# RWKV-7 and a hard-swish feed-forward on one core: unit 4's r loaded later, unit 8 prepared one block later

## The chip, the cores and the metric

The kernel runs on one core of a Trainium2 chip. The metric is the device time of one execution in microseconds (us). A measurement is the median of several runs; the profile is of one further execution.

## What is computed

First a recurrence over 768 steps for each of 4 x 8 heads of 40 features, then a feed-forward over the 3072 rows that it gives. The state is a 40 x 40 matrix for each head.

```python
for t in range(S):                     # B, H, S, D = 4, 8, 768, 40
    y[:, :, t] = einsum('bhd,bhde->bhe', r[t], state)
    Sa = einsum('bhde,bhe->bhd', state, a[t])
    state = state * w[t] - Sa (outer) b[t] + v[t] (outer) k[t]
x = y.transpose(0, 2, 1, 3).reshape(B * S, H * D)         # 3072 x 320
h = x @ w_in                                               # 320 -> 2048
out = (h * clip(h + 3, 0, 6) / 6) @ w_out                  # 2048 -> 320
```

## The kernel before

**Units and groups.** The sequence is cut into chunks of 64 steps. A unit is one chunk of one pair of batches with all 8 heads: 24 units, numbered 0 to 23, in six groups of four (`NU = 4`). Within a chunk the recurrence is written as matrix products, which needs the inverse of a triangular 64 x 64 matrix for each head.

**Preparation of a unit** (`prepare`): stages that do not need the state. `W` turns w on TensorE (L506), evicts it (L595, L599) and scans it on VectorE (L603); `gam` makes the cumulative products and their reciprocals (L612 to L635). `A` and `B` turn a and b and scale them (L528 or L506, L516, L650, L658). `F` is the matrix to be inverted (L672 or L685, evicted at L676 or L692 and L695). `factor` turns the reciprocals (L705, L710), evicts them as rgt (L714, L717), and GpSimd scales k and b by them (KBt, L725). `K`, `E`, `EV` follow (L736, L554 with the mask L578, L752 with the eviction L757).

**Inversion** (`invert`): for each group, some 60 small VectorE instructions (L804, L810) on all four units' F, two transposes (L813, L818), and copies into tinv (L825, L826). The other 32 x 32 blocks come from matrix products, two per half group (`third_block`: L839, evicted at L847, then L862, evicted at L872).

**A unit's own step** (`step`): `RT`, `VT` (r and v turned: L531 and L516), `fade` (the state decays, L913), `R` (L927, L931), `C` (L554, L578), `S` (L949), `U`, `UT` (L968, L1007), `rS` (L1023), `H`, `ysn` (L1064, then L1071 to L1074: outputs and the new state), `move` and `move2` (DMAs of the outputs into xt, L1111 and L1116).

**Feed-forward** (`feed_forward`): 48 jobs, two for each unit. `expand` computes h (L1171; L1184 in another shape), the activation makes gt (L1193 on ScalarE, L1194 on VectorE), `contract` computes o (L1219), and ob goes to memory (L1243). These jobs are dealt out in pieces (`pieces`, `feed`) between the stages of the recurrence. Each engine runs its instructions in the order in which the program writes them down, so where a piece stands is fixed.

**Loads.** `fetch` issues a unit's loads on SyncE's queue: two DMAs for W, B or K (L490), four for V (L487), and for r of unit 4 and later eight and for a of unit 8 and later four (L478). A load is written down where the tile that it overwrites has been read for the last time: W of the next unit in the stage `W`, A in `A`, B and K in `factor`, r of the next unit in `RT`. Units from 8 on share one tile for each of W, A, B and K. SyncE handles its queue in order; an instruction that waits holds up those behind it.

**Order.** (1) The first group is prepared, and the matrices w_in and w_out are loaded and converted. (2) `PLAN` is a list of lines by hand: the steps of units 0 to 3. From its line 10 (`BEGIN`) the second group, units 4 to 7, is prepared beside it by the generator `by_twos`, one `next` per line; its remaining rounds are run after the plan. (3) The inversion of the second group is finished under 18 rounds of 1.25 feed-forward pieces each. (4) From then on the units 4 to 23 each take four blocks; blocks are counted from `m = 0`. Unit 4's `RT` and `VT` stand ahead of block 0, unit 5's in block 3; `R`, `C`, `S` of unit 4 are in block 1, `U`, `UT`, `rS` in block 2, `H` in block 3, `ysn` in block 4, `move` in block 5; and so on, four blocks later for each unit.

In (4) `begins` gives the block in which the preparation of a unit starts. Where the next unit's preparation starts less than four blocks later, the five blocks are

```python
    CLOSE_STAGES = [["W", "gam"], ["A", "B"], ["F", "K", "factor"], ["E"], ["EV"]]
```

`a_block(m)` sorts what is due in block m into two parts: own steps, and preparations that started in a block divisible by 4, go into the first; the other preparations go into the second. Half of the block's feed-forward pieces stand between the parts and half behind them. The third-block products of a group (`block`) stand behind the second part of the first two blocks of its first and of its second unit: L839 in the one, L862 in the other.

`together` runs a part: first the TensorE halves of all its stages, in the order of `PRODUCTS`, then the remaining halves (evictions, VectorE and GpSimd work, loads) in the order of `RESULTS`. PSUM for this is one single bank (`one`) and two pairs of banks (`pair`), which stages share as far as their widths allow (512 columns a bank); if a part needs more than five banks, what has begun is finished first.

```python
    PRODUCTS = ["W", "S", "K", "VT", "B", "factor",
                "ysn", "EV", "R", "C", "U", "UT", "rS", "H", "E", "F"]
    RESULTS = ["ysn", "W", "VT", "EV", "R", "S", "C", "A", "B", "move", "move2", "open",
               "U", "UT", "rS", "F", "K", "fade", "H", "E", "factor", "RT", "gam"]
```

Of the kernel before, what the change touches and what calls it, by code (L numbers as in the profile page):

```python
# [31 lines left out]
def kernel(  # L32
# [47 lines left out]
    NU = 2 * NP  # L80
# [30 lines left out]
    def begun_ffn():  # L111

        lent.__exit__(None, None, None)
        pairs.clear()
        pairs.append(("pair", 2))
        pools["h"] = ctx.enter_context(tc.tile_pool(name="hidden", bufs=1, space=PSUM))
# [70 lines left out]
    AHEAD, FAR = NU + 1, 2 * NU - 1  # L187
# [6 lines left out]
    def second(name):  # L194

        tag = {"B": "S", "K": "U"}[name]
        return padded(grp.tile([P, H, SLOT], F32, name=name + "1", tag=tag, bufs=1), name)

    def seconds():
        t = inv.tile([P, 2, H, SLOT], F32, name="WA1", tag="x", bufs=1)  # L200
        for i, name in enumerate("WA"):
            others[name] = padded(t[:, i], name)
# [244 lines left out]
    NK = NG * NU  # L447
# [3 lines left out]
    def fetch(name, i, engine=None):  # L451

        if i is None or i >= NK:
            return
        x, crossed = {"W": (w, 0), "A": (a, 0), "B": (b, 0), "K": (k, 0), "R": (r, 1),
                      "V": (v, 1)}[name]
        if name == "V":
            t = values[i % AHEAD]
        else:
            t = placed.get((name, i))  # L460
            if (name, i) == ("R", 1):
                t = others["K"]
            if (name, i) == ("W", NU + 1):
                t = values[NU]
            t = t if t is not None else (others if i < 2 * NU and i % 2 and name != "R" else inputs)[name]
        g, p = names[i]
        engines = engine or nc.sync
        if name == "R" and i >= NU or name == "A" and i >= 2 * NU:
            y = x[2 * p:2 * p + 2, :, g * BL:(g + 1) * BL, :]
            n = 2 if name == "R" else 1  # L470
            y = y.rearrange("q (k s j) t e -> s j (q k) (t e)", s=2, j=n).rearrange(
                "s j k (l e) -> s j l k e", e=2 * D)
            for s in range(2):
                for c in range(0, D, L):
                    z = s * SLOT + c
                    to = rooms[name][z:z + L].rearrange("l (j k e) -> l j k e", j=n, e=2 * D)
                    for j in range(n):
                        nc.sync.dma_start(out=to[:, j, :, 0:2 * D - c], in_=y[s, j, :, :, c:])  # L478
            data[i][name + "N"] = t
            return  # L480
        for q in range(2):
            engine = engines[q] if isinstance(engines, tuple) else engines
            y = x[2 * p + q, :, g * BL:(g + 1) * BL, :]
            rows = slice(q * BL, (q + 1) * BL)
            if crossed:
                for s in range(2):
                    engine.dma_start(out=t[rows, 4 * s:4 * s + 4, 0:D],  # L487
                                     in_=y[s::2].rearrange("h t e -> t h e"))
            else:
                engine.dma_start(out=t[rows, :, 0:D], in_=y.rearrange("h t e -> t h e"))  # L490
        data[i][name + "N"] = t
# [761 lines left out]
    def pieces(n):  # L1253

        owed[0] += n * (8 / 9 if spread[0] else 1)
        while owed[0] >= 1:
            owed[0] -= 1
            if not next(stream):
                owed[0] = 0.0

    def aside(n, weight=0):

        for _ in range(n):
            if side and next(side[0], side) is side:
                side.popleft()
            due[0] += weight
            while due[0] >= 1:
                due[0] -= 1
                next(weights, None)
# [6 lines left out]
    def run(stage, steps=0, mixed=0, deals=0):  # L1276

        for at in stage:
            if at == DONE:
                return  # L1280
            aside(steps, mixed)
            deal(deals)
# [26 lines left out]
    def by_twos(first, steps, mixed, rate):  # L1309


        chains = [by_stages(first + i, prepared(first + i)) for i in range(NU)]
        for t in range(TWOS):

            order = [0, 1] if t < STAGES else []
            order += [2, 3] if t > 5 else []
            if t < 2:
                order = [0, 1, 0, 1][4 * t:]
            if t == 3:
                order = [2, 0, 3, 1]  # L1320
            for i in order:
                if t >= 2 or first != NU:
                    run(chains[i], steps if t > 10 else 0, mixed, 1 if t < 5 else 0)
                pieces(rate / 2)
            if t == 10:
                side.append(invert(group_F[-1], third, first == 0))
            yield
# [88 lines left out]
    for t, line in enumerate(plan):  # L1416
        if t == 8:
            begun_ffn()
            ring.clear()
            ring.extend([("one", 1), ("whole", 2)])  # L1420
        for name, *amounts in line:
            run(chains[name[0]], 0, 0, *map(int, amounts))
        limit[0] = {3: 15, 8: 17, 9: PIECES}.get(t, limit[0])
        if t == BEGIN - 2:
            seconds()
            third.clear()
            second_group = by_twos(NU, 3, 0, 1.25)
        if t == BEGIN:
            fetch("A", NU + 1)
            fetch("W", NU + 3)  # L1430
        if t == BEGIN + 2:
            fetch("V", NU)
            fetch("V", NU + 1)
            fetch("R", NU)
        if t == BEGIN + 1:

            for name in "BK":
                others[name] = second(name)
                fetch(name, NU + 1)
        if t >= BEGIN - 2:  # L1440
            pieces(3 if t < BEGIN else 1.5 if t < BEGIN + 3 else 0)
        if t >= BEGIN:
            next(second_group)
    for _ in weights:
        pass
    for _ in second_group:
        pass
    for _ in range(18):
        aside(3)
        pieces(1.25)  # L1450
# [18 lines left out]
    BLOCKS = 4  # L1469
# [33 lines left out]
                     for stage in stages[name])  # L1503
        finish()

    begins = {u: max(3 * (u - 2 * NU), BLOCKS * (u - NU - AHEAD)) for u in range(2 * NU, NK)}
    coming, ahead, own = deque(range(2 * NU, NK)), {}, {}

    def a_block(m):
# [95 lines left out]
```

## Time and profile before

| | before |
|---|---|
| median of 3 runs | 773.58 us (771.44 to 774.97) |
| the profiled execution | 772.7 us; its span, first to last instruction, 771.0 us |
| TensorE (PE) busy | 710.8 us, 92% |
| VectorE (DVE) busy | 508.8 us, 66% |
| ScalarE (ACT) busy | 310.4 us, 40% |
| GpSimd (POOL) busy | 150.8 us, 20% |
| mean granted TensorE clock | 0.956 of full speed |
| DMA | 48.43 MB in 175999 packets, mean 63 GB/s |

All positions below are microseconds from the start of the profiled span. The first two parts of the order above end at about 166 us, the third at about 190 us; the blocks fill the rest up to the last jobs. In rows of a timeline the columns are start, duration, engine, line, operation, what it writes and reads, shape and count; in brackets stands the idle time of the engine before it and what ended it. SPq is SyncE's queue; its rows are the issuing of DMAs, not their transfer.

### The profile page before, as it was taken

The page shows a single profiled execution, that of the slowest core. Times are in us where ns is not written, and L with a number is a line of the kernel's source. Part 1 is how long each engine was busy: PE and PEld are TensorE (multiplying, and loading weights), DVE is VectorE, ACT ScalarE, POOL GpSimd, SP SyncE. Part 2 cuts the span into 40 slices and gives each one's busy share as a digit, 9 for nine tenths or more (in the row PEclk, how much of TensorE's full clock was granted, in tenths as well). Part 3 has the DMA queues.
Part 4 walks back from the last instruction along what each step waited for, and adds up shares of the span by engine and source line. Part 5 has one row for each costly group of instructions (what it writes and reads, how often), then busy time and mean ns, then how long its engine had stood idle before and what let it go on. Part 6 is the DMA issues. An engine that isn't in the chain of part 4 may idle for free.

```text
span 771.0 us, 33034 instructions
## 1 busy us (share of the span) xinstructions
PE 710.8 (92%) x14568; PEld 603.1 (78%) x14568; DVE 508.8 (66%) x1027; ACT 310.4 (40%) x644; POOL 150.8 (20%) x303
## 2 busy tenths in 40 slices
PE   4635888999899989999999999999999999999997
PEld 3534777778779778888888888888888888888885
DVE  8899968588557799556798456898436982333210
ACT  2377865232553324552434453234444224322211
POOL 7403210321322211212112121203112010000000
PEclk7956799999999999999999999999999999999999
DMA  9685563420334322233322223313331110110000
GB/s 124 119 179 150 114 170 57 79 43 18 64 65 84 70 55 48 52 71 60 64 52 55 53 62 63 69 37 60 57 72 42 25 24 23 35 35 12 14 16 19
DMA packets 175999, 48.43 MB, mean 63 GB/s; under 512 B 159216, under 2 KB 174576, under 8 KB 175856
## 3 DMA queue, kind: packets, MB, share of 16 engines
q1 hardware_dynamic: 171552, 45.58, 29.7%
q8 instruction: 115, 1.88, 1.0%
q10 hardware_dynamic: 4304, 0.74, 0.7%
q14 instruction: 28, 0.23, 0.1%
HBM read 37.62 MB, written 3.93 MB: 54 GB/s over the span
## 4 chain that ended last, share of the span: by engine, by line
PE 77%; DVE 8%; SPq 5%; issue 3%; DMA 3%; ACT 3%; POOL 0%; DVEq 0%; ACTq 0%; POOLq 0%
PE o L1219 25%; PE h L1171 24%; PE pair L554 4%; PE pair L1064 4%; SPq L490 3%; PE h L1184 2%; PE one L506 2%; PE pair L968 2%; PE pair L927 1%; DVE prod L804 1%; PE pair L1007 1%; PE pair L516 1%; PE pair L752 1%; DVE x L810 1%; PE pair L1023 1%
## 5 line engine op out<-in xcount | busy, mean ns | idle before, releaser
L1171 PE MATMUL h<-xt,win 128*128 128x128 f32 (+1 forms) x2000 | 229.2, 282 | 3.0 <-DVE gt L1194 3.0
L1219 PE MATMUL o<-wout,gt 128*128 128x320 f32 x768 | 230.4, 443 | 0.0
L1171 PEld LDWEIGHTS h<-xt,win 128*128 128x128 f32 (+1 forms) x2000 | 212.9, 193 | 17.5 <-issue 3.1
L1219 PEld LDWEIGHTS o<-wout,gt 128*128 128x128 f32 x768 | 138.6, 190 | 50.3 <-issue 0.2
L1193 ACT ACTIVATE gt<-h,three 128x512 f32<-128x512 f32 x96 | 62.6, 686 | 110.3 <-PE h L1171 88.0
L1194 DVE SCALAR_TENSOR_TENSOR gt<-gt,h 128x512 f32<-128x512 f32 x96 | 61.8, 679 | 62.4 <-ACT gt L1193 62.3
L578 DVE COPY_PREDICATED area<-mask,pair 128x512 f32<-128x512 int32 x56 | 40.5, 726 | 55.2 <-PE pair L554 36.7
L804 DVE TENSOR_TENSOR prod<-x 128x30 f32<-128x30 f32 (+9 forms) x180 | 64.1, 356 | 8.9 <-POOL x L789 3.3
L810 DVE TENSOR_TENSOR x<-x,prod 128x30 f32<-128x30 f32 (+9 forms) x180 | 63.0, 350 | 5.5
L725 POOL TENSOR_TENSOR KBt<-K,rgt 128x320 f32<-128x320 f32 x22 | 19.1, 866 | 142.2 <-ACT rgt L714 134.2
L1071 DVE TENSOR_TENSOR ys<-pair,ys 128x512 f32<-128x512 f32 x20 | 13.8, 690 | 40.5 <-PE pair L1064 40.5
L993 POOL COPY area<-V 128x320 f32<-128x320 f32 x20 | 9.1, 454 | 149.6 <-DVE area L645 53.7
L757 ACT ACTIVATE EV<-pair 64x320 f32<-64x320 f32 x44 | 19.0, 432 | 39.2 <-PE pair L752 38.9
L1064 PE MATMUL pair<-area,KBt 64*64 64x104 f32 x1280 | 32.4, 250 | 0.0
L1237 ACT ACTIVATE ob<-o 128x320 f32<-128x320 f32 x22 | 9.6, 435 | 56.6 <-PE o L1219 35.2
L603 DVE TENSOR_TENSOR_SCAN prods<-area,start 128x528 f32<-128x528 f32 x24 | 29.9, 1250 | 3.4 <-ACT area L599 3.3
L632 POOL COPY gam<-prods 128x256 f32<-128x256 f32 x24 | 12.7, 531 | 99.1 <-DVE prods L603 99.1
L614 DVE TENSOR_TENSOR_SCAN area<-area,start 128x528 f32<-128x528 f32 x24 | 30.6, 1276 | 0.8
L1064 PEld LDWEIGHTS pair<-area,KBt 64*64 64x64 f32 x1280 | 29.9, 133 | 1.5 <-issue 1.4
L872 ACT ACTIVATE tinv<-pair 32x256 f32<-32x256 f32 x48 | 18.0, 375 | 31.9 <-PE pair L862 31.3
L931 DVE TENSOR_TENSOR RR<-pair,EV 128x320 f32<-128x320 f32 x22 | 10.7, 485 | 20.9 <-PE pair L554 13.6
L633 POOL COPY rgam<-prods 128x256 f32<-128x256 f32 x22 | 23.9, 1084 | 0.0
(289 smaller groups left out, 1078.5 us busy)
## 6 DMA issues: line engine op xcount, KB each, us to landing
V<-in_v_dram SPq DMA_DIRECT2D x96, 40.0 KB
out_dram<-ob SPq DMA_DIRECT2D x47, 80.0 KB
R<-in_r_dram SPq DMA_DIRECT2D x92, 40.0 KB
B<-in_b_dram SPq DMA_DIRECT2D x42, 80.0 KB
K<-in_k_dram SPq DMA_DIRECT2D x42, 80.0 KB
W<-in_w_dram SPq DMA_DIRECT2D x37, 80.0 KB
A<-in_a_dram SPq DMA_DIRECT2D x37, 80.0 KB
xt<-yg SPq DMA_DIRECT2D x72, 40.0 KB
```

What stands on the lines that cost most here:

```text
L554: nc.tensor.matmul(out=o[i][half(q), n ^ (2 * q * placed), :], lhsT=lhs[half(i, D), n ^ (2 * q * swap), half(q)], rhs=rhs[half(i, D), n, h ...
L578: nc.vector.copy_predicated(out=x[:].rearrange("p (i h) t -> p i h t", i=2), mask=mask8, data=o[2])
L603: nc.vector.tensor_tensor_scan(out=prods[:].rearrange("p r m i -> p (r m i)"), data0=wm[:, 0:SCAN], data1=start[:], initial=0.0, op0=ALU.m ...
L614: nc.vector.tensor_tensor_scan(out=back, data0=back, data1=start[:], initial=0.0, op0=ALU.mult, op1=ALU.add)
L633: nc.gpsimd.tensor_copy(rv[:, :, 0:HB], o["prods"][:, :, 0, 0:HB][:, :, ::-1])
L804: nc.vector.tensor_tensor(out=pv, in0=_ap(x[:], (i + 1) * L + i, [[L, n], [0, i]]), in1=_ap(x[:], i * L, [[0, n], [1, i]]), op=ALU.mult,)
L810: nc.vector.tensor_tensor(out=rest, in0=rest, in1=pv, op=ALU.add)
L1064: nc.tensor.matmul(out=both[q][half(s), pr, :], lhsT=o[name][half(q), h * D:h * D + SLOT], rhs=beside[name][half(q), 4 * rs + 2 * (s ^ (q ...
L1171: nc.tensor.matmul(out=hp[c][:, i, :], lhsT=lhsT, rhs=rhs, start=(begun[c] == 0), stop=(begun[c] == 3 * NQ - 1))
L1193: nc.scalar.activation(out=gt[:], in_=hp[c][:], func=AF.Relu, bias=three[:], scale=1.0)
L1194: nc.vector.scalar_tensor_tensor(out=gt[:], in0=gt[:], scalar=6.0, in1=hp[c][:], op0=ALU.min, op1=ALU.mult)
L1219: nc.tensor.matmul(out=op[:], lhsT=gts[c][:, n, :], rhs=wout[:, c * HJ + r * NQ + n, :], start=((split or r == 0) and c == 0 and n == 0), ...
```

## The change

Two edits. The load of r for unit 4 (`fetch("R", NU)`, eight DMAs) is taken from the plan's line 12, where it stood behind the loads of v for units 4 and 5, and is written down behind the last round of `by_twos`, ahead of the 18 rounds of feed-forward pieces. And `begins` of unit 8 becomes 1 instead of 0; those of the other units (3, 6, 9, 12, ...) stay. With that unit 8's five stages stand in blocks 1 to 5 and in their second parts (1 is not divisible by 4), instead of in the first parts of blocks 0 to 4.

```diff
         if t == BEGIN + 2:
             fetch("V", NU)
             fetch("V", NU + 1)
-            fetch("R", NU)
...
     for _ in second_group:
         pass
+    fetch("R", NU)
     for _ in range(18):
         aside(3)
         pieces(1.25)
...
-    begins = {u: max(3 * (u - 2 * NU), BLOCKS * (u - NU - AHEAD)) for u in range(2 * NU, NK)}
+    begins = {u: max(3 * (u - 2 * NU), BLOCKS * (u - NU - AHEAD), 1) for u in range(2 * NU, NK)}
```

## The prediction

> **What bounds the kernel now.** The page came first: TensorE is busy for 92% of the span and carries 77% of the chain that ended last. The second view, busy time in chosen stretches, says where TensorE's order alone decides. Columns: stretch and length, then busy time and count of PE, PEld, DVE, ACT, POOL, then granted clock, DMA share, GB/s.
>
> ```profile
> PE 77%; DVE 8%; SPq 5%; issue 3%; DMA 3%; ACT 3%; POOL 0%; DVEq 0%; ACTq 0%; POOLq 0%
> ```
>
> ```profile
> 147.42:150.83 3.41, 1.73 (x14) 1.37 (x13) 0.69 (x1) 0.48 (x2) 0.00 (x0) 1.00 0.58 98
> ...
> 161.07:164.48 3.41, 1.91 (x68) 1.56 (x68) 3.24 (x6) 0.49 (x2) 3.06 (x5) 1.00 0.13 24
> 164.48:167.90 3.42, 3.42 (x41) 2.48 (x40) 3.18 (x10) 1.23 (x3) 0.00 (x0) 0.50 0.46 80
> ...
> 277.12:280.54 3.42, 1.51 (x17) 1.32 (x20) 3.25 (x10) 0.00 (x0) 0.07 (x1) 1.00 0.00 0
> 280.54:283.95 3.41, 3.41 (x42) 3.13 (x43) 3.20 (x7) 1.92 (x4) 1.32 (x4) 0.50 0.38 81
> 290.00:758.00 468.00, 468.00 (x9381) 399.31 (x9380) 278.32 (x564) 171.73 (x372) 74.18 (x137) 1.00 0.23 46
> ```
>
> From 290 us on TensorE never stops, so its remaining work there is fixed, and the change can act only through TensorE's idle time before 290. The other pairs show that a stretch with TensorE idle for 1.5 to 1.9 us was twice followed by 3.4 us at half clock, and once (the first line, 1.7 us idle) not.
>
> Third, SyncE's and TensorE's timelines, and one row of the chain of waits, around what is moved.
>
> ```profile
> 129.51 3.93 SPq L478 DMA_DIRECT2D R<-in_r_dram  x8
> ...
> 144.12 1.35 SPq L490 DMA_DIRECT2D B<-in_b_dram  x2
> ...
> 146.94 1.90 SPq L490 DMA_DIRECT2D B<-in_b_dram  x2
> ...
> 163.82 1.27 SPq L490 DMA_DIRECT2D K<-in_k_dram  x2
> 177.16 11.11 SPq L1243 DMA_DIRECT2D out_dram<-ob  x4
> ```
>
> ```profile
> 148.21 2.59 DMA B<-in_b_dram
> ```
>
> ```profile
> 148.93 0.63 PE L506 MATMUL one<-ident,B 128*128 128x128 f32 x4 [1.30 <-DMA B<-in_b_dram]
> ...
> 150.93 0.63 PE L506 MATMUL pair<-ident,B 128*128 128x128 f32 x4 [0.48 <-DMA B<-in_b_dram]
> ...
> 199.84 0.75 PE L862 MATMUL pair<-zs,tt 32*32 32x32 f32 x64 [1.21 <-DVE area L645]
> ...
> 205.60 0.69 PE L1023 MATMUL pair<-RT,S 40*64 40x64 f32 x32 [1.10 <-ACT UT L1013]
> ...
> 212.43 0.60 PE L506 MATMUL one<-ident,W 128*128 128x128 f32 x4
> ...
> 218.42 0.46 PE L516 MATMUL pair<-ident,B 64*128 64x64 f32 x8
> ```
>
> SyncE issues almost without a pause from 124 to 158 us. Unit 4's r is in the middle of that, and TensorE waits 1.30 and 0.48 us for the b of units 6 and 7 issued behind it. The next two gaps, 1.21 and 1.10 us, lie in the first blocks of the second half, where unit 8's preparation stands. The last two rows are unit 9's W and b.
>
> **The r load.** Eight DMAs, 3.93 us of SyncE, leave the queue ahead of A, W, unit 3's xt moves, B, K and V. Everything behind comes up to 3.9 us earlier. What those loads wait for allows it: GpSimd's last read of the old b's (KBt, 136.63 and 138.33 us) is over before the new issue times, 140.2 and 143.0. Unit 7's b landed at 148.21 + 2.59 = 150.80; it will land near 146.9, and TensorE, with both gaps closed, asks for it at 149.1. So 1.78 us go and 2.3 us of slack remain; the work behind (transposes, F, then the inversion on VectorE up to 187.7) follows TensorE directly and shifts with it. **-1.8 us**, at worst 0 if other loads take the place.
>
> The load itself now stands behind unit 8's K (issued by 165.09) and ahead of the first output store, which sits in the queue until 177.16 for a contraction that starts at 172.08. SyncE is idle in between: issue near 165, 1.76 us from the last issue to landing (the chain's later R row), read at 194.71. 20 us of cover. Were it behind the stores instead (188.3), it would land near 194, still about in time. Cost nothing.
>
> **Unit 8, one block later.** Its stages keep their instructions, but move from the first half of blocks 0 to 4 (merged with unit 4's and 5's steps) to the second half of blocks 1 to 5 (merged with unit 9's preparation, which still begins at block 3).
>
> *What goes.* Unit 8's scans no longer stand on VectorE between RT (194.71) and the mask that frees the PSUM pair for L862 (199.07): the 1.21 us go. Without K and the factor transposes in front, U, UT and rS fit the five banks together, so rS need not wait for UT's eviction: 1.10 us go. **-2.3 us**, at worst 0.
>
> *The b of unit 9.* All units from 8 on share one b buffer. Unit 9's load is issued when unit 8's factor stage has read it. That was block 2, two blocks ahead of its use in block 4; now it is block 3. In TensorE's order from unit 9's W to unit 9's B stand, by starts in its timeline, W 0.44, K 0.53, the factor transposes 0.39, F 0.6, a feed-forward piece 1.18, ysn 1.47 and two pieces 2.35: asked for after 7.0 us. (Before, with other work between, 5.99, the last two rows above.) The load's path has prices from unit 9's own turn:
>
> ```profile
> 225.16 0.37 ACT L692 ACTIVATE F<-pair 32x256 f32<-32x256 f32 x1 [3.19 <-PE pair L685]
> ...
> 227.25 0.44 ACT L714 ACTIVATE rgt<-pair 128x320 f32<-128x320 f32 x1
> ```
>
> F's matmuls end 2.0 us after W begins; F's six evictions 2.1 (225.16 to 227.25), rgt 0.44, KBt twice 0.86, so the buffer is free at 6.3. Unit 6's r and unit 10's W are issued ahead of it, but they end by then. Two issues 1.35, landing 2.0 (unit 7's b) to 3.4 us (unit 6's: issued by 145.47, used at 148.93) after the second: 9.7 to 11.1, or 11.5 with one slow issue as in the 146.94 row. TensorE waits 2.7 to 4.5 us with all of its queue behind: unit 8's E, L839, the feed-forward pieces. I take **+3.0**, near the quicker landing since SyncE's neighbours there are few; below 0 it can't be.
>
> *Block 5.* Unit 8's EV now shares a PSUM pair with unit 9's factor transposes, which pushes F into the second pair. L862 of the next third block follows at once and needs one of the two: F's, free after EV's evictions (0.88, ScalarE's row at 216.21) and F's 2.1, or the other, after rgt. F's matmuls run 0.6 beside that: 0.88 + 2.1 - 0.6 + 0.1 for the hand-over. Before, F shared with the factor and L862 at 225.03 took a free pair. **+2.5 us**, from 0 (the allocator finds a free pair after all) to 2.9 (it picks the other).
>
> *The clock.* Two waits of 2.5 to 3.0 us are longer than those that twice brought the half clock. What the one from 164.48 cost, by TensorE's rows: a job's 48 h matmuls 5.51 instead of 4.83 (166.64 against 176.50), four o matmuls 1.88 instead of 1.34 (163.81 against 159.73), EV 1.09 instead of 0.68 (165.62 against 163.21): 1.6 us. Between 0 and two of them; I take one: **+1.6**. [...]
>
> Sum: -1.8 - 2.3 + 3.0 + 2.5 + 1.6 = +3.0 us. The profiled execution took 772.7 (span 771.0 and 1.7 around), 0.9 below the median of three, 773.58; what is added is the same on either: 775.7 and **776.6**. A measurement can tell about 0.5% here, 3.9 us, so this counts as no change.
>
> **Rivals.**
> *Late b with a slow clock twice (slower).* The same two waits, unit 9's b taking the long landing (4.5) and both waits followed by half clock (3.2): -4.1 + 4.5 + 2.5 + 3.2 = +6.1, 779.7. It decides from a b wait of 4 us on. For it: unit 6's landing of 3.4, the two half-clock rows. [...] 0.22.
> *The clock holds.* +1.4, 775.0. [...] 0.17.
> *One wait only.* If L862 finds a free pair, -4.1 + 3.0 and half a clock loss of 0.8: -0.3, 773.3. For it: the L862 before (199.84) waited for a mask alone although an older reader of the other pair was still to come, so the allocator chooses. 0.13.
> *The blocks have room (faster).* If unit 9's b also lands in time, nothing but gains: -4.1, 769.5. It needs the factor's chain of 6.3 us and the load's 3.4 to fit 7.0; the rows speak against it. 0.08.
> *The forecast* has the rest, 0.40, with its own range of +1.0 to +4.6 (774.6 to 778.2).
>
> **How the numbers follow.** Over 3.9 us slower: the first rival and a fifth of the forecast's share, 0.30. Over 3.9 us faster: most of the last rival and a little for gains that I don't see, 0.08. The rest, 0.62. The range from 770.5 to 780.0 leaves out the last rival and the worse half of the first, and takes in some spread of single runs (771.44 to 774.97).
>
> **What would show it.** Right: R (L478) issued near 163 and SyncE idle until the stores; no idle before L506 of B near 147; W (L506 one) of unit 8 after R and C, not before L839; L862 of the first third block and rS without a gap; then a gap at L516 of B, released by DMA, near 213 to 217, one of 2.5 us at the second L862, released by ACT; half clock behind one of them. Wrong: no gap at that L516 (the b path is shorter than I add up), no gap at L862 (other PSUM pairs), gaps left near 147, or any TensorE idle after 290.

## The result, and the profile after

| | before | changed |
|---|---|---|
| median, runs side by side | 772.73 us (5 runs, 770.95 to 774.97) | 780.6 us (5 runs, 778.2 to 780.95) |
| ratio, with its 95% interval | | 1.0092 (1.0065 to 1.012) |
| the profiled execution | 772.7 us, span 771.0 | 780.8 us, span 779.1 |

The change is slower, by 0.92%. A second measurement of the same kernel, further down, gave 1.0066 (1.0041 to 1.0092). The intervals overlap; the loss is 5 to 7 us by the two ratios. The forecast was +3.0 us, called no change; the measured 780.6 us lies just above the range of 770.5 to 780.0, nearest to the rival "late b with a slow clock twice".

The page's chain of work that ended last, shares by engine:

```profile
PE 73%; DVE 10%; SPq 6%; issue 5%; DMA 2%; ACT 2%; POOL 1%; DVEq 0%; POOLq 0%; ACTq 0%
```

TensorE's part of the chain fell from 77% to 73%. But this chain runs through the start of the kernel too, which differs by some us from one execution to the next (unit 4's A transposes begin at 124.82 us in the one profile and at 126.53 in the other, so 1.7 of the 8.1 us between the two spans lie ahead of both edits' places); the changed kernel without unit 8's edit also shows 73%, and it is not slower. So this line cannot carry the verdict, and the places are needed. SyncE's queue, the issuing of DMAs:

```profile
164.88 5.06 SPq L478 DMA_DIRECT2D R<-in_r_dram  x8
175.56 11.70 SPq L1243 DMA_DIRECT2D out_dram<-ob  x4
...
213.96 1.27 SPq L490 DMA_DIRECT2D B<-in_b_dram  x2
```

TensorE's timeline (the bracket is the idle time ahead of the row, and what ended it):

```profile
149.41 0.60 PE L506 MATMUL one<-ident,B 128*128 128x128 f32 x4
...
193.87 0.66 PE L949 MATMUL one<-ident,state 128*128 128x128 f32 x4 [0.42 <-DVE state L913]
...
197.26 0.75 PE L862 MATMUL pair<-zs,tt 32*32 32x32 f32 x64
...
200.90 0.65 PE L1023 MATMUL pair<-RT,S 40*64 40x64 f32 x32
...
207.34 0.60 PE L506 MATMUL one<-ident,W 128*128 128x128 f32 x4
...
216.73 0.29 PE L516 MATMUL pair<-ident,B 64*128 64x64 f32 x1 [2.11 <-DMA B<-in_b_dram]
217.27 0.68 PE L516 MATMUL pair<-ident,B 64*128 64x64 f32 x7 [0.24 <-DMA B<-in_b_dram]
...
230.33 1.03 PE L862 MATMUL pair<-zs,tt 32*32 32x32 f32 x64 [2.58 <-ACT F L695]
```

The r load stands at 164.88, behind K and ahead of the stores. The gaps ahead of the b of units 6 and 7, of the first L862 and of rS have gone; a small one of 0.42 us at the state is new. Two large ones have come: 2.11 and 0.24 us for unit 9's b, and 2.58 us at the second L862. ScalarE's rows ahead of that:

```profile
227.32 0.87 ACT L757 ACTIVATE EV<-pair 64x320 f32<-64x320 f32 x2 [3.39 <-PE pair L752]
...
229.63 0.65 ACT L695 ACTIVATE F<-pair 32x256 f32<-32x256 f32 x2
```

EV's evictions first, then F's, which end at 230.28; L862 begins at 230.33. The granted clock around the two waits (columns as in the prediction: PE, PEld, DVE, ACT, POOL, granted clock, DMA share, GB/s):

```profile
213.38:216.79 3.41, 1.30 (x6) 0.66 (x4) 2.78 (x6) 0.00 (x0) 1.87 (x4) 1.00 0.53 92
216.79:220.20 3.41, 3.17 (x105) 2.68 (x106) 1.05 (x2) 0.05 (x1) 0.00 (x0) 0.50 0.67 128
220.20:223.62 3.42, 3.42 (x24) 2.20 (x26) 0.27 (x1) 1.73 (x5) 0.00 (x0) 0.50 0.14 44
227.03:230.45 3.42, 0.83 (x61) 0.70 (x57) 0.00 (x0) 3.04 (x9) 0.00 (x0) 1.00 0.17 25
230.45:233.86 3.41, 3.41 (x69) 2.56 (x66) 0.49 (x1) 1.79 (x5) 2.35 (x4) 0.50 0.03 7
290.00:758.00 468.00, 466.28 (x9462) 397.43 (x9461) 282.81 (x578) 172.72 (x376) 74.15 (x137) 1.00 0.23 46
```

Each of the two waits is followed by half clock (0.50), the first by 6.83 us of it (216.79 to 223.62) and the second by 3.41 (230.45 to 233.86). The last line is not full: TensorE paused once for 1.72 us, at 326.50, where ScalarE also stood still (2.01 us) and the profile names no releaser. The prediction named any TensorE idle time after 290 us as a sign of being wrong. But in the second profile of the changed kernel TensorE is busy for all of 290 to 750, and one of the experiments (part 6, r at its old place) has a pause of 1.84 us at 317.80, ahead of the very same matmul: both have run 5794 matmuls by then. So the pause seems to belong to a place in the program and comes in some executions only; it is not taken for an effect of the change, and what holds TensorE there stays open.

**Where the time lies.** To leave out the start, the spans between fixed instructions of TensorE's timeline were compared: from the A transposes of unit 4 to the F of units 6 and 7 (the stretch of the r load), from there to VT of unit 4 (the last preparations and the third step of the order), from VT of unit 4 to U of unit 5 (blocks 0 to 5), and what follows to the end.

| kernel | unit 4's A to F of 6, 7 | F to VT of unit 4 | blocks 0 to 5 | rest |
|---|---|---|---|---|
| before | 29.53 | 35.97 | 37.74 | 542.90 |
| changed | 27.59 | 34.61 | 46.17 | 544.18 |
| changed, measured again | 27.59 | 34.61 | 46.56 | 542.30 |

So the first edit gives 1.9 us, and blocks 0 to 5 lose 8.4 to 8.8. The rest differs by 1.3 us, no more than the pause, so nothing of the loss is won back further on. The second column differs by 1.36 us, and that is luck of the profiles. A wait for a mask stands there in both, and only before is it followed by half clock (0.50 from 164.48 to 167.90, four o matmuls in 1.88 us instead of 1.34; in the changed kernel the granted clock is 1.00 from 160 to 190). The kernel before:

```profile
163.21 0.68 PE L752 MATMUL pair<-V,area 64*64 64x40 f32 x32 [1.50 <-DVE area L578]
163.81 1.88 PE L1219 MATMUL o<-wout,gt 128*128 128x320 f32 x4
```

The changed kernel:

```profile
162.95 0.68 PE L752 MATMUL pair<-V,area 64*64 64x40 f32 x32 [1.59 <-DVE area L578]
163.56 1.34 PE L1219 MATMUL o<-wout,gt 128*128 128x320 f32 x4
```

It does not follow r's place: with r at its old place that row takes 1.34 us in the first profile of the second edit alone and 2.50 us in its second, behind waits of 1.46 and 1.60 us.

### The profile page after: what moved, and what is told of

It reads as the page before. It is cut to its first block, busy times and chain, and to the rows that moved or that the text cites. A ratio compares the mean times of both kernels' runs of the same rounds, so it can differ in the third digit from the quotient of the medians.

```text
span 779.1 us, 33028 instructions
## 1 busy us (share of the span) xinstructions
PE 713.7 (92%) x14568; PEld 604.0 (78%) x14568; DVE 508.9 (65%) x1027; ACT 310.6 (40%) x644; POOL 149.5 (19%) x303
## 3 DMA queue, kind: packets, MB, share of 16 engines
q8 instruction: 115, 1.88, 1.0%
## 4 chain that ended last, share of the span: by engine, by line
PE 73%; DVE 10%; SPq 6%; issue 5%; DMA 2%; ACT 2%; POOL 1%; DVEq 0%; POOLq 0%; ACTq 0%
PE o L1219 24%; PE h L1171 23%; PE pair L554 4%; PE pair L1064 3%; PE h L1184 2%; DVE prod L804 2%; DVE x L810 2%; SPq L490 2%; PE one L506 2%; PE pair L927 2%; SPq L487 1%; PE pair L968 1%; PE pair L516 1%; PE pair L1007 1%; PE pair L1023 1%
## 5 line engine op out<-in xcount | busy, mean ns | idle before, releaser
L1219 PE MATMUL o<-wout,gt 128*128 128x320 f32 x768 | 233.6, 448 | 0.0
L1219 PEld LDWEIGHTS o<-wout,gt 128*128 128x128 f32 x768 | 140.6, 193 | 51.7 <-issue 2.2
```

Of the source, the lines that this page charges most:

```text
L1219: nc.tensor.matmul(out=op[:], lhsT=gts[c][:, n, :], rhs=wout[:, c * HJ + r * NQ + n, :], start=((split or r == 0) and c == 0 and n == 0), ...
```

## The experiments

The theory: the first edit gains as predicted; the second costs two waits, for unit 9's b and for a PSUM pair at the second L862, and each wait costs again through the half clock seen behind it. The rivals: the loss comes from the second parts of the blocks as such (what shares a part with what), not from the later start; or the waits only take time that is lost anyway further on; or the r load at its new place costs something. All ratios are against the kernel before, run on the same chip at the same time, in 5 rounds; the diffs are against the changed kernel.

**1. Each edit alone.** The first edit alone keeps `begins` as before:

```diff
-    begins = {u: max(3 * (u - 2 * NU), BLOCKS * (u - NU - AHEAD), 1) for u in range(2 * NU, NK)}
+    begins = {u: max(3 * (u - 2 * NU), BLOCKS * (u - NU - AHEAD)) for u in range(2 * NU, NK)}
```

> Only the first edit: unit 4's r loaded behind the second group's preparation; unit 8 begins at block 0 as before. Theory (all of the loss comes from unit 8's later start: two TensorE waits and the half clock behind them): the two gaps for the b of units 6 and 7 near 149 us are gone, nothing waits for r, 1.8 us faster than the kernel before, 771 where that takes 772.7. Rival (the late load of r costs something in the blocks, or shifts the loads behind it): no gain or slower, 773 to 776, with TensorE or VectorE waiting for a DMA between 165 and 230 us.

Measured: 772.46 us, ratio 0.9974 (0.9955 to 0.9993). The gaps for the b of units 6 and 7 are gone, those at the first L862 and at rS (1.20 and 1.10 us) are still there, no new wait appears. The second edit alone puts the load back:

```diff
             fetch("V", NU + 1)
+            fetch("R", NU)
...
-    fetch("R", NU)
```

> Only the second edit: unit 8 begins at block 1; unit 4's r stays where it was. Theory: the whole loss and none of the gain, the changed kernel plus 1.8: 782.4, some 9.7 above the kernel before, with a gap of 2 to 3 us at unit 9's B (released by DMA), one of 2.6 at the second L862 (released by ScalarE's F), and half clock behind them. Rival (the two edits do it together, unit 4's r being late in SyncE's queue): within 2 us of the kernel before.

Measured: 780.32 us, 1.0063 (1.004 to 1.0087), +5.4 us by the medians where +9.7 was expected. Its profile has both waits (2.06 + 0.36 and 2.59 us) and half clock behind both, and 46.12 us in the blocks. The places were right and the sum too large; whether the two edits add up was therefore asked again later.

**2. TensorE kept busy during the waits.** Transposes of the identity, whose result nobody reads, stand ahead of unit 9's B and ahead of the second L862. They shorten no wait; they only keep TensorE from being idle in it.

```diff
+    def fill(n):
+        t = bank("one", [P, 512], 1)
+        for _ in range(n):
+            nc.tensor.transpose(out=t[:, 0:P], in_=ident[:], identity=ident[:])
...
         def b_stage():
+            if i == 2 * NU + 1:
+                fill(18)
...
+            if i == NU + 1 and j == 1:
+                fill(22)
             run(blocks[i])
```

> The changed kernel, with TensorE kept busy through the two waits: 18 transposes of the identity ahead of unit 9's B and 22 ahead of the second L862, about 2.0 and 2.4 us of work whose result nobody reads; they add work and leave nothing out. Theory (the half clock behind the waits costs 5 us, more than the waits themselves in excess of those removed): the waits last as long as before, but the granted clock stays at full from 190 to 280 us, and the time falls by 4 to 5 us to 775.5 to 776.5. Rival (the slow rows there have another cause, or the clock halves for another reason): 780 to 781, as the changed kernel, or slower by the added work of up to 4.4 us.

Measured: 775.43 us, 1.0008 (0.9987 to 1.0029), in the range expected for the time; by the ratios that is 4.5 to 6.5 us below the two measurements of the changed kernel. The stretches of this kernel:

```profile
190.00:225.00 35.00, 34.52 (x810) 27.70 (x809) 23.03 (x43) 15.32 (x37) 10.16 (x20) 1.00 0.34 66
225.00:270.00 45.00, 44.96 (x988) 38.28 (x989) 27.11 (x52) 21.90 (x53) 11.18 (x24) 1.00 0.36 67
```

The granted clock is 1.00 in both stretches, and both pieces of real work are as late as before: unit 9's B begins 9.34 us after its W (9.39 in the changed kernel), the second L862 3.26 us after F (3.26). The blocks take 41.65 us instead of 46.17: the clock alone was 4.5 us of the loss, more than either wait, and nearly three times the 1.6 of the prediction.

**3. Each wait taken away at its cause.** Unit 8's K and factor one block earlier, so that unit 9's b is loaded two blocks ahead of its use again:

```diff
+    EIGHTH = [["W", "gam"], ["A", "B", "K", "factor"], ["F"], ["E"], ["EV"]]
...
-            ahead[u, m] = prepared(u), CLOSE_STAGES if close else AHEAD_STAGES
+            ahead[u, m] = prepared(u), EIGHTH if u == 2 * NU else CLOSE_STAGES if close else AHEAD_STAGES
```

> The changed kernel, with unit 8's K and factor stages moved one block forward (into block 2, beside its A and B), so that unit 9's b and k are issued two blocks ahead of their use again; its EV still meets unit 9's F in block 5. Theory: the gap at unit 9's B (2.4 us) and the 3.4 us of half clock's loss behind it vanish; the L862 wait of 2.6 us and its 1.7 us of half clock stay: 5.5 us faster than the changed kernel, about 775. Rival (the b isn't late because of the buffer but because SyncE's queue is full): the gap stays at 1 us or more and the time at 778 or above.

Measured: 774.6 us, 0.9993 (0.9973 to 1.0013), as expected. TensorE's timeline:

```profile
214.52 0.46 PE L516 MATMUL pair<-ident,B 64*128 64x64 f32 x8
...
225.00 1.07 PE L862 MATMUL pair<-zs,tt 32*32 32x32 f32 x64 [2.59 <-ACT F L695]
```

No gap at B, the other wait whole. That one was now followed by half clock (0.50) from 224.10 to 230.92, 6.8 us instead of the 3.41 in the changed kernel; its last 0.9 us already lay in the slow stretch.

Then the second L862 behind the feed-forward pieces that follow it, with the late b left as it is:

```diff
-            if i % NU < 2 and j < 2:
+            late = (i, j) == (NU + 1, 1)
+            if i % NU < 2 and j < 2 and not late:
...
             feed(rate / 2, inversion)
+            if late:
+                block(i, j)
```

> The changed kernel, with the second L862 of the second group (block 5) written down behind the two feed-forward pieces that follow it instead of ahead of them; all work stays. Theory: the two pieces (2.3 us) run while ScalarE evicts EV and F, so the wait of 2.6 us shrinks to under 0.5 and its half clock (1.7 us) goes; the wait at unit 9's B (2.4 us) and its 3.4 us of half clock stay: some 4 us faster than the changed kernel, 776 to 777 where that takes 780.6. Rival (the L862 wait is not bound to the PSUM pair but to the third block's operands): the wait stays, 780.

Measured: 776.34 us, 1.0035 (1.0015 to 1.0055), as expected. TensorE's timeline:

```profile
229.69 0.75 PE L862 MATMUL pair<-zs,tt 32*32 32x32 f32 x64 [0.24 <-ACT F L695]
```

The wait for the pair was covered by the 2.4 us of o matmuls ahead of it, at the price of 0.54 us at rS, which needs tinv soon after. A later place would have covered late operands as well, so the time alone does not decide against the rival; the releaser does (F's eviction, which is no operand of L862), and so does part 4, where the wait goes though L862 and its operands are left alone. The wait at B stayed (2.08 + 0.42 us).

**4. Both waits taken away.** As the factor in block 2 frees the b in time, so E in the same part as F leaves EV to stand alone, without F behind it:

```diff
-    EIGHTH = [["W", "gam"], ["A", "B", "K", "factor"], ["F"], ["E"], ["EV"]]
+    EIGHTH = [["W", "gam"], ["A", "B", "K", "factor"], ["F", "E"], ["EV"]]
```

(the older line is that of the first kernel of part 3; both edits of the change are in.)

> The changed kernel, with unit 8's preparation drawn together into four blocks: W and gam in block 1; A, B, K and factor in block 2; F and E in block 3; EV in block 4. Theory: both waits and all the half clock behind them vanish, the two older waits (1.21 and 1.10 us) stay away and unit 4's r keeps its gain: 4 us faster than the kernel before (0.995 of it), no TensorE gap over 0.5 us between 165 and 265 us. Rival (the fuller blocks 2 to 4 bring a wait of their own, for VectorE's masks or the second pair of PSUM banks): a new gap of 1 to 2 us there and half clock behind it, no better than the kernel before.

Measured: 768.76 us, 0.9936 (0.9915 to 0.9958). It is faster than both kernels, by 5.0 us than the kernel before (3.2 to 6.6), where 4 was expected. Its timeline and stretches:

```profile
213.63 0.46 PE L516 MATMUL pair<-ident,B 64*128 64x64 f32 x8
...
220.88 0.75 PE L862 MATMUL pair<-zs,tt 32*32 32x32 f32 x64
```

```profile
165.00:200.00 35.00, 34.59 (x502) 28.84 (x504) 29.95 (x69) 11.39 (x23) 7.07 (x11) 1.00 0.15 31
200.00:260.00 60.00, 59.60 (x1376) 49.14 (x1370) 38.96 (x72) 28.36 (x69) 13.36 (x30) 1.00 0.39 76
```

From 165 to 260 us there is neither wait, no half clock (1.00 in both lines), and the later start is kept: TensorE is idle for 0.8 us in 95. The blocks take 36.40 us, against 37.74 before. So what the later start removes is worth 1.3 us in the blocks, where the prediction had 2.3.

**5. The second parts without the later start.** Unit 8 begins in block 0 again, but its stages stand in the second parts:

```diff
-    begins = {u: max(3 * (u - 2 * NU), BLOCKS * (u - NU - AHEAD), 1) for u in range(2 * NU, NK)}
+    begins = {u: max(3 * (u - 2 * NU), BLOCKS * (u - NU - AHEAD)) for u in range(2 * NU, NK)}
...
-    parts[(u, begin) in ahead and begin % BLOCKS > 0].setdefault(name, []).append(fs[name])
+    parts[(u, begin) in ahead and (begin % BLOCKS > 0 or u == 2 * NU)].setdefault(name, []).append(fs[name])
```

> The first edit, and unit 8 beginning at block 0 as before, but with all five of its blocks' stages in the second part of the block. Theory: unit 9's b keeps nearly two blocks, EV stays away from unit 9's F, and U, UT and rS stay together, so rS doesn't wait (1.10 us gone); W's scans are still on VectorE ahead of the mask, so some of the 1.21 us stays: 3 us faster than the kernel before (0.996). Rival (what made the change slow is the second parts as such, not the later start): unit 9's B or an L862 waits 2 us and more, 776 or above.

Measured: 773.5 us, 0.9994 (0.9974 to 1.0015). This expectation was missed: neither of the two large waits is there, and the gap at rS is gone, but the gain is not. TensorE's timeline:

```profile
198.62 0.74 PE L862 MATMUL pair<-zs,tt 32*32 32x32 f32 x64 [1.60 <-DVE area L578]
199.29 3.40 PE L1171 MATMUL h<-xt,win 128*128 128x128 f32 x16
```

Unit 8's scans (194.09 to 196.9 us on VectorE) still stand between RT and the mask (197.76) that frees the pair for the first L862. The wait of 1.60 us is followed by half clock: the 16 h matmuls take 3.40 us instead of the 2.05 that the same row has in the faster kernel of part 4. So the two large waits do not come from the second parts as such; nor do they come from the later start as such, since the kernel of part 4 starts as late and has neither. They come from what the later start pushed back: factor into block 3, so that unit 9's b is loaded late, and EV into block 5, beside unit 9's F. The wait at the first L862 goes only if the scans start later.

**6. Do the edits add up?** The kernel of part 4 with r loaded at its old place:

> Unit 8 in four blocks from block 1, as in the kernel before that one in this call, but unit 4's r loaded where it was at first. Theory (the two edits act apart from each other): 1.8 to 2 us slower than with r moved, 2 us faster than the kernel before (0.997), with the gaps of 1.3 and 0.5 us near 149 us back. Rival (the r load's place only matters together with unit 8's): the same time as with r moved.

Measured: 771.8 us, 0.9969 (0.995 to 0.9989), as expected; of the two gaps only one is back, 0.56 us at unit 7's b. Against 0.9936 the r load's new place is worth 0.33%. Then the changed kernel and the second edit alone once more, side by side:

> The changed kernel once more, beside its second edit alone on the same chip. Theory (the edits act apart): 1.8 to 2 us faster than the second edit alone, as the r load's move gave alone and with unit 8 in four blocks; 6 to 7 us above the kernel before. Rival (what r gives is lost where unit 8 begins late): the same time as the second edit alone, or slower.

Measured: 779.01 us, 1.0066 (1.0041 to 1.0092), waits of 2.03 + 0.41 and 2.59 us. That is 5.1 us above the kernel before, where 6 to 7 was expected.

> The second edit alone, once more. Theory: 8 to 9 us above the kernel before. Rival: 5 to 6, as its first measurement, and no slower than both edits together.

Measured: 782.98 us, 1.0099 (1.0065 to 1.0133). The difference of the two is 0.33% again. The two measurements of the second edit alone, 1.0063 and 1.0099, lie apart; these runs spread from 778.99 to 787.65. Part of that spread can be seen. With r at its old place the wait for unit 7's b is 0.48 us before, 1.01 and 0.56 in two experiments and 2.05 in the profile of this run (787.5 us), where slow rows follow it (8 h matmuls in 1.92 us instead of 1.06) and the stretch from unit 4's A to F takes 32.01 us instead of 29.53. With 0.26% in part 1, three comparisons give 2.0 to 2.6 us for the first edit, whether unit 8 is late or not; the two differences of 0.33% are each uncertain by about as much as they say, and only the 0.26% was measured directly against the kernel before.

**7. What each slow stretch costs.** The transposes of part 2, only ahead of unit 9's B, and only ahead of the second L862:

> The changed kernel, TensorE kept busy only through the wait for unit 9's b (18 transposes of the identity ahead of its B, whose result nobody reads). Theory: that wait's window drops and so do two half-clock windows (6.8 us, 3.4 us of loss), the one behind L862 stays: 3 to 3.5 us faster than the changed kernel. Rival (L862's wait alone brings the slow clock, the windows behind b are noise of the profile): under 1 us faster.

Measured: 777.51 us, 1.0032 (1.0013 to 1.0052), 0.34% or 2.6 us below the changed kernel measured beside it, where 3 to 3.5 was expected.

> The changed kernel, TensorE kept busy only through the wait of the second L862 (22 transposes of the identity ahead of it, whose result nobody reads). Theory: one half-clock window less, or two where the wait straddles a border of windows: 1.7 to 3 us faster than the changed kernel; the two windows behind unit 9's b stay. Rival: no gain, or slower by what the transposes take beyond the wait.

Measured: 778.24 us, 1.0054 (1.0035 to 1.0073), 0.12% or 0.9 us below, where 1.7 to 3 was expected. The blocks in the two profiles are shorter by 1.8 and 2.5 us (44.75 and 44.10 against 46.56). Both add up to 3.5 to 4.3 us, near the 4.5 of part 2, but times and profiles put the larger half in different places. The split is not settled: one of these intervals is 1.5 us wide to each side, and how much slow work follows the same wait differs from run to run. In the profile of the first of the two kernels the wait at L862 (2.59 us) was followed by more of it than in the changed kernel (the eight o matmuls behind it 4.63 us instead of 3.68, U 1.09 instead of 0.68), so that less was left of its gain.

## Why the prediction was right or wrong

**The r load: right.** -1.8 foreseen; -1.9 in the profile, 2.0 to 2.6 in three comparisons. Nothing was lost at the new place: eight issues from 164.88 to 169.94, and SyncE free until the stores at 175.56.

**What goes in the blocks: right in place, too large.** The gaps of 1.21 and 1.10 us went, as named, but the faster kernel of part 4, which has the same removals and no new wait, is only 1.3 us shorter in the blocks. 0.4 us came back at once at the state (193.87), which VectorE and GpSimd deliver no earlier for TensorE's having less to do ahead of it (from VectorE's L813 to its L913 6.56 us before, 6.58 here); the rest, 0.6 us, is not idle time: the same 876 matmuls between VT of unit 4 and U of unit 5 are busy for 35.99 us there and for 35.42 before. Why they take longer in the other order was not traced.

**The b of unit 9: right.** Foreseen: asked for after 7.0 us from unit 9's W, there after 9.7 to 11.1, +3.0 taken. In the profile TensorE asks at 214.62, 7.3 us after W at 207.34; KBt frees the buffer at 213.94 (6.6, foreseen 6.3), the two issues take 1.27, and the landing is 2.04 us behind them at 217.27 (9.9). The upper end of that forecast, with one slow issue, adds up to 11.6 us and not 11.5; nothing hangs on it. TensorE is idle for 2.35; by the starts of the neighbours (from the o matmuls ahead of B to the row behind B: 5.68 us against 2.75 in the kernel of part 4) 2.9, since B's own transposes come apart.

**The second L862: right.** Foreseen 2.5, from EV's evictions, then F's. Measured 2.58, by the very rows.

**The clock: this step failed.** It was priced at one stretch of 1.6 us, "between 0 and two of them". Half clock came behind both waits, 6.83 us behind the first and 3.41 behind the second: three times the 3.4 us that were priced, 4.0 to 4.5 us of loss in all. The price of one was near enough (1.3 to 1.5 each; the one priced from 164.48 cost 1.36 by the table above, since the 1.6 added durations of rows that overlap); the number of them was not. In the timelines, from the row behind B to unit 9's F the changed kernel takes 9.19 us and the kernel of part 4 6.22, and 0.5 more with E, which stands elsewhere there: 2.5 us. From the second L862 to U 4.57 against 3.03: 1.5. Together 4.0, and 4.5 by part 2. The prediction took a slow stretch for 3.4 us long, because the one that it had priced, from 164.48 to 167.90, was. There TensorE was busy all the time (3.42 of 3.42 us). Here the wait runs on into the slow time: the line 216.79 to 220.20 of the changed kernel has 3.17 of 3.41 us busy, and the next is slow too. It is the same in the second kernel of part 7 (3.15 of 3.40 us from 217.90, then 3.40 at 0.50 again) and at the L862 of part 3's first kernel (2.51 of 3.41 us from 224.10, then 3.41 at 0.50 again). But in the changed kernel's second profile the slow rows reach as far (from B's at 215.92 into VT's, 0.79 us at 222.64) without a pause among them. Why the slow time was twice as long there is not shown. The rival with two slow stretches was the right one in that, and wrong in its other condition: it asked for a b wait of 4 us, and 2.35 were enough. That its +6.1 us come so near is luck: its b wait is 1.6 too large, its gains 0.9 too large and its clock 0.8 to 1.3 too small.

With the measured terms the sum is -1.9 - 1.3 + 2.9 + 2.6 + 4.0 = +6.3 us, between the two measurements (+5.1 and +7.1). The chance of 0.30 for slower was too small as well: the prediction's own rows had half clock behind 1.5 us of idle time, and the one counter-row, 1.7 us without a drop, was weak ground for halving the price of two waits that were each longer. Of the rivals, "the clock holds", "one wait only" and "the blocks have room" each have their condition refuted by the rows above.

## What to carry to other kernels

A wait of TensorE can cost more than its length: here 4.9 us of waiting brought another 4.0 to 4.5 through the clock, so a move that trades two small gaps of 1.1 and 1.2 us for two of 2.4 and 2.6 loses twice. Where a preparation starts later, look at what its last reader releases: the load of the next tile behind a shared buffer, and the PSUM pair that the next product needs; moving those stages alone (K and factor into block 2, E beside F, EV into block 4) kept the gain and made the kernel, with the r load moved too, 0.64% faster than before. A load that nobody needs soon should leave an in-order queue at the point where other loads are late: that gave 0.3% by itself. And when two single profiles are compared, look whether the same wait was followed by half clock in the one and not in the other, as at 163 us here, before the difference is put down to the edit.

## What the runs showed of the chip

The granted clock fell to 0.50 behind these waits of TensorE. The kernel before: 1.50 us at 163.21 (161.07 to 164.48 busy for 1.91 of 3.41 us), then 0.50 for 3.42 us. The changed kernel: 2.11 and 0.24 us at unit 9's B, then 0.50 for 6.83 us; 2.58 us at the second L862, then 0.50 for 3.41 us. The first kernel of part 3: 2.59 us at the same L862, and 0.50 for 6.8 us, of which the wait's last 0.9 are a part. Behind these it stayed at 1.00: 1.30 and 0.48 us at the b of units 6 and 7 before (147.42 to 150.83 busy for 1.73 of 3.41 us; 1.00 up to 156 us); 1.59 us at 162.95 in the changed kernel; and 2.69 us at 107.88 before and 2.67 us at 108.83 in the changed kernel, longer than either of the two waits that the change brought. So in these runs the length of a wait alone did not tell whether half clock followed, or for how long, and what else decides is not shown.

The filler of unread transposes in part 2 is the same from the other side: with it the clock was 1.00 from 190 to 270 us, and the blocks took 4.5 us less. It is not a cure: taking the waits away at their cause gave 0.72% more (1.0008 against 0.9936), 5.6 us.
